# Where tiles start in SBUF: matmul operands at one place modulo 256 bytes, the gated halves staggered by 64

## The chip, the cores and the metric

The kernel runs on one core of a Trainium2 chip. The metric is device time in microseconds for one execution of the whole program. Each kernel's time is the median of several executions; the profile is of one further execution, taken by the hardware profiler. Its span runs from the first to the last instruction of the program, and the execution's own time is a little longer than its span.

## What is computed

A small two-way attention between tokens and state slots, followed by a gated feed-forward block with a three-tap convolution along the sequence. B, H, S, Ns, D are 8, 8, 512, 32, 64; the feed-forward block takes 512 features to 1024 and back.

```
scores = x @ state^T / 8;   a  = softmax(scores);   xread = a  @ state
scores2 = state @ x^T / 8;  a2 = softmax(scores2);  sread = a2 @ x
y = concat([xread, sread], axis=sequence)           # (B, 544, 512)
h = relu(y @ w_in)
conv = conv_w[0]*h[t-1] + conv_w[1]*h[t] + conv_w[2]*h[t+1]
out = (h * sigmoid(conv)) @ w_out
```

## The kernel before

All work is recorded as operations of one engine each (a matmul group, an activation, a vector operation, a load), and a table of numbers, `ORDER`, sets the order in which they are issued. No scheduler decides anything at build time, and each engine runs its list in that order, waiting on semaphores where an operand isn't ready.

The feed-forward block takes nearly all the time. It runs in 64 steps, i = 8b + f, for batch b and slice f of 128 of the 1024 hidden features. In a step:

- `hidden` (L579) multiplies: the stationary operand is a 128x128 piece of `u` (state times `w_in`), the moving operand 128x512 of `a` (the softmax). Both are kept as a high and a low half in float32r, `u0`/`u1` and `a0`/`a1`, and `PASSES` runs three products: u1 by a0, u0 by a1, u0 by a0, each over two groups, so six matmuls a step. In batch 0 plain float32 is used instead (L574, operands `u` and `p`).
- ScalarE applies relu into a tile `h` (L584), multiplies by the middle tap into a tile `t` (L601); VectorE adds the two other taps (L605, L610); ScalarE takes a tanh (L614); VectorE forms the gated value (L619).
- the gated value is split into halves `g0` (ScalarE, L178 through `gate_high`) and `g1` (VectorE, L181 through `gate_low`).
- `project` (L637 in `product`) multiplies: the stationary operand is a 128x128 piece of `g0` or `g1`, the moving one 128x512 of `wo` (the high or the low half of `w_out`), three passes for each of four chunks of the sequence, so twelve matmuls a step. The first four steps use plain float32 (L645, moving operand `whole`, stationary `t`). The same `product` serves the state rows (`gts` for `acc_t`) and the last chunk of batch 0 (`last` for `acc_c`).

In every matmul call the second argument is the stationary operand, which a LDWEIGHTS record (engine PEld in the profile) loads, and the third is the moving one, which the MATMUL record (engine PE) streams:

```
PE.matmul(acc, g[j][:, cs], wo[:, k, f, :], ...)          # L637
PE.matmul(ps_h[i], u[j][:, g, fs], a[k][:, g, :], ...)    # L579
```

There are 708 MATMULs of `g` with `wo`, 48 of `gts`, 24 of `last`, and 336 of `u` with `a`: 1116 in float32r, all with a stationary operand of 128 columns and a moving one of 512.

SBUF tiles come out of two pools, `keep` (one buffer for good) and `work` (a tag's buffers used in turn; `SBUF` gives their number: four `g0`, four `g1`, four `h`). A pool lays its tiles one after another in the order in which their tags first appear, so a tile's address follows from the sizes of those ahead of it. Two small sizes matter for what follows: `cw` is 96 bytes in a partition, and a tile `h` is 513 floats, 2052 bytes, and takes 2080.

Of the kernel before, what the change touches and what calls it, by code (L numbers as in the profile page):

```python
# [9 lines left out]
F32 = mybir.dt.float32  # L10
F32R = mybir.dt.float32r
# [4 lines left out]
P = 128  # L16
B, H, S, NS, D = 8, 8, 512, 32, 64
NP = H // 2
NG = H // 4
NCH = S // P  # L20
DM, DFF = 512, 1024
NK = DM // P
NF = DFF // P
T = S + NS

LOTS = ((0, 1, 2, 3), (4, 5, 6, 7))
# [16 lines left out]

SBUF = dict(hc=3, xt=4, xx=2, at=5, e2=2, e2t=2, af=1, a=2, u=2, h=4, t=5, g=4, ss=1,
            rr=2, nm2=4, s2=4, s1=4, o=2, gts=2)

RAW = ("a0", "a1", "u1")
PSUM = dict(acc=4, ph=2, ps=2)
# [103 lines left out]
def fused_kernel(ctx: ExitStack, tc: tile.TileContext, xT, xn, stT, w_in, conv_w, w_out, out):  # L152
    nc = tc.nc
    V, A, G, PE = nc.vector, nc.scalar, nc.gpsimd, nc.tensor

    psum = ctx.enter_context(tc.tile_pool(name="psum", bufs=4, space=bass.MemoryType.PSUM))
    keep = ctx.enter_context(tc.tile_pool(name="keep", bufs=1))
    work = ctx.enter_context(tc.tile_pool(name="work", bufs=2))

    def bank(name, tag="ps"):  # L160
        return psum.tile([P, 512], F32, tag=tag, name=name, bufs=PSUM[tag])

    def buf(shape, dtype, tag, name, pool=work, **kw):
        return pool.tile(shape, dtype, tag=tag, name=name, bufs=SBUF.get(tag) or SBUF[tag[:-1]], **kw)

    ident = keep.tile([P, P], F32, name="ident")
    make_identity(nc, ident)
    cw = keep.tile([P, NF, 3], F32, name="cw")
    wi = keep.tile([P, NK, DFF], F32, name="wi")
    wo = keep.tile([P, 2, NF, DM], F32R, name="wo")  # L170

    st = keep.tile([P, B * NP, NS], F32, name="st")

    sr = [keep.tile([P, NP, len(lot) * NS], F32, name=f"sr_{m}") for m, lot in enumerate(LOTS)]


    def high(hi, src):
# [24 lines left out]
    def w_tile(j, tag, *more):  # L202
        shape = [P, *pieces[j][0].shape[1:], *more]
        return buf(shape, U32, tag, f"{'raw' if more else tag}_{j}",
                   padded_shape=[P, *([1, 512] if j == W_CONV else shape[1:3]), *more])
# [18 lines left out]
    def w_sign(j):  # L224
        dst = pieces[j][1]
        if dst is None:
            f = j - W_OUT
            whole[f] = buf([P, DM], F32, f"g{f % 2}", f"whole_{f}")
            dst = whole[f].unsqueeze(1)
        V.scalar_tensor_tensor(dst.bitcast(U32), raws.pop(j)[:, :, :, 1], 0x80000000, hcs.pop(j),  # L230
                               op0=ALU.bitwise_and, op1=ALU.bitwise_or)
# [27 lines left out]
    at, ps_s, nm2, e2, ps_t, e2t, s2, ps_r, rr, ps_f, xts, xxs = ({} for _ in range(12))  # L259

    def xt_load(i):
        b, g = divmod(i, NG)
        xts[i] = buf([P, 2, S], F32, "xt", f"xt_{i}")
        nc.sync.dma_start(xts[i], xT[b, :, 2 * g:2 * g + 2, :])  # L264
# [99 lines left out]
    af, s1, av = {}, {}, {}  # L364
# [182 lines left out]
    corner = keep.tile([P, NF, 3], F32, name="corner")  # L547
    corner2 = keep.tile([P, NF, 3], F32, name="corner2")
    corners = keep.tile([P, 1, NF], F32, name="corners")
    last = keep.tile([P, NF, P], F32, name="last")  # L550

    def at_step(i):
        b, f = divmod(i, NF)
# [326 lines left out]
```

## Time and profile before

| | |
|---|---|
| median of three runs | 376.81 us |
| the three runs | 375.97, 378.32, 376.81 us |
| the profiled execution | 376.16 us |
| its span | 374.4 us |
| matmul records | 2418, as many weight loads |

How to read the profile's rows: in a row of a group stand the line, the engine, the operation, the tile written and the tiles read, the shape and the number of instructions. Matmul records overlap: each lasts from its start to the modelled end of its pipeline, so the time that one matmul takes from the engine is the distance from its start to the next one's start. The chain of work that ended last cuts its pieces at these starts, so that a piece's length divided by its count gives this distance.

### The profile page before, as it was taken

How to read it: one execution, taken by the hardware profiler on the slowest of the kernel's cores; microseconds unless marked ns; L12 is line 12 of the kernel's file. 1: busy time of each engine (PE TensorE's matmuls, PEld its weight loads, DVE VectorE, ACT ScalarE, POOL GpSimd, SP SyncE). 2: the span in 40 equal slices, each digit the busy share in tenths (PEclk: the TensorE clock that was granted, in tenths of full speed). 3: DMA queues.
4: the chain of work that ended last, by engine and by line, in shares of the span. 5: the costliest groups of instructions: out<-in, count | busy, mean ns of one | idle time of the engine just before them, and what ended most of it. 6: DMA issues, size and time to landing. Idle time of an engine off the chain costs nothing.

```text
span 374.4 us, 6509 instructions
## 1 busy us (share of the span) xinstructions
PE 362.8 (97%) x2418; PEld 267.4 (71%) x2418; DVE 309.2 (83%) x540; ACT 265.7 (71%) x536; POOL 44.2 (12%) x158
## 2 busy tenths in 40 slices
PE   7988989999999999999999999999999999999994
PEld 6852446677668776877888877877778778888883
DVE  1988999999999989989989898786787578666951
ACT  3898998866789689766765658666766477558632
POOL 1002102310121120102010011011311121011000
PEclk9999999999999999999999999999999999999998
DMA  7999984033310445000010011100020001002004
GB/s 257 326 355 312 379 290 166 0 114 100 141 43 2 144 141 190 34 2 4 28 56 2 0 56 58 56 4 15 13 86 0 28 30 56 2 0 86 3 0 168
DMA packets 21728, 35.05 MB, mean 94 GB/s; under 512 B 1600, under 2 KB 14272, under 8 KB 21696
## 3 DMA queue, kind: packets, MB, share of 16 engines
q1 hardware_dynamic: 21696, 34.63, 27.0%
q8 instruction: 19, 0.31, 0.4%
q14 instruction: 13, 0.11, 0.1%
HBM read 25.71 MB, written 8.91 MB: 92 GB/s over the span
## 4 chain that ended last, share of the span: by engine, by line
PE 89%; DMA 7%; SPq 2%; ACT 0%; issue 0%; ACTq 0%
PE acc L637 45%; PE ps_h L579 21%; PE ps_hs L560 4%; PE ps_u L494 4%; PE acc_t L637 3%; DMA raw<-w_in 3%; DMA st<-stT 3%; PE ps_h L574 2%; PE acc L645 2%; PE ps_r L318 2%; PE ps_s L277 2%; DMA xx<-xn 2%; PE acc_c L637 1%; PE ps_t L305 1%; SPq L209 1%; SPq L264 0%
## 5 line engine op out<-in xcount | busy, mean ns | idle before, releaser
L637 PE MATMUL acc<-wo,g 128*128 128x512 f32 x708 | 179.9, 400 | 0.0
L637 PEld LDWEIGHTS acc<-wo,g 128*128 128x128 f32 x708 | 131.0, 188 | 43.3 <-issue 8.4
L579 PE MATMUL ps_h<-a,u 128*128 128x512 f32 x336 | 85.7, 397 | 0.0
L579 PEld LDWEIGHTS ps_h<-a,u 128*128 128x128 f32 x336 | 62.4, 188 | 15.9 <-issue 1.7
L605 DVE SCALAR_TENSOR_TENSOR t<-h,cw,t 128x511 f32<-128x511 f32 x64 | 47.1, 744 | 11.0 <-ACT t L601 10.8
L584 ACT ACTIVATE h<-ps_h 128x512 f32<-128x512 f32 x64 | 37.8, 594 | 19.6 <-PE ps_h L579 12.9
L614 ACT ACTIVATE t<-t 128x512 f32<-128x512 f32 x64 | 39.6, 627 | 15.3 <-DVE t L610 15.2
L610 DVE SCALAR_TENSOR_TENSOR t<-h,cw,t 128x512 f32<-128x512 f32 (+1 forms) x64 | 47.3, 745 | 1.7 <-POOL h L589 0.5
L619 DVE SCALAR_TENSOR_TENSOR t<-t,h 128x512 f32<-128x512 f32 (+1 forms) x64 | 42.2, 666 | 5.8 <-ACT t L614 5.6
L181 DVE TENSOR_TENSOR g<-t,g 128x512 fp32r<-128x512 f32 (+1 forms) x60 | 40.2, 674 | 7.4 <-ACT g L178 7.1
L178 ACT ACTIVATE g<-t 128x512 fp32r<-128x512 f32 (+1 forms) x60 | 37.0, 621 | 11.9 <-DVE t L619 8.1
L601 ACT ACTIVATE t<-h,cw 128x512 f32<-128x512 f32 x64 | 44.7, 719 | 0.1
L589 POOL COPY h<-hs 128x1 f32<-128x1 f32 x56 | 20.3, 372 | 172.2 <-DVE t L619 141.9
L594 POOL COPY hs<-h 128x1 f32<-128x1 f32 x64 | 19.0, 315 | 120.3 <-ACT h L584 120.2
L651 ACT ACTIVATE o<-acc 128x512 f32<-128x512 f32 (+1 forms) x30 | 17.1, 584 | 11.6 <-PE acc L637 11.3
L181 DVE TENSOR_TENSOR u<-ps_u,u 128x512 fp32r<-128x512 f32 x28 | 18.6, 679 | 3.9 <-ACT u L178 3.9
L178 ACT ACTIVATE u<-ps_u 128x512 fp32r<-128x512 f32 x28 | 16.1, 594 | 4.2 <-PE ps_u L494 4.1
L188 PE MATMUL idle<-ident 128*128 128x128 f32 x102 | 14.8, 306 | 1.8 <-POOL ident masks.py:199 1.8
L560 PEld LDWEIGHTS ps_hs<-sr,wi 128*128 128x128 f32 x128 | 15.7, 191 | 1.2 <-ACT sr L333 0.4
L188 PEld LDWEIGHTS idle<-ident 128*128 128x128 f32 x102 | 13.7, 216 | 3.5 <-POOL ident masks.py:199 1.8
L213 ACT ACTIVATE hc<-raw 128x512 f32<-128x512 f32 (+1 forms) x17 | 11.1, 652 | 6.8 <-DMA raw<-conv_w 4.4
L560 PE MATMUL ps_hs<-sr,wi 128*128 128x128 f32 x128 | 15.7, 275 | 0.0
(88 smaller groups left out, 394.1 us busy)
## 6 DMA issues: line engine op xcount, KB each, us to landing
xt<-xT SPq DMA_DIRECT2D x16, 512.0 KB, 6.5
xx<-xn SPq DMA_DIRECT2D x16, 512.0 KB, 5.2
out<-o SPq DMA_DIRECT2D x30, 256.0 KB, 2.1
raw<-w_in SPq DMA_DIRECT2D x8, 512.0 KB, 7.1
raw<-w_out SPq DMA_DIRECT2D x8, 512.0 KB, 7.8
out<-o_t SPq DMA_DIRECT2D x8, 64.0 KB, 1.7
st<-stT SPq DMA_DIRECT2D x1, 448.0 KB, 10.4
out<-o_c SPq DMA_DIRECT2D x1, 256.0 KB, 6.7
```

The source lines that it names most:

```text
L178: A.activation(hi, src, AF.Copy)
L181: engine.tensor_tensor(lo, src, hi.bitcast(F32), op=ALU.subtract)
L188: PE.matmul(idle[0][:, :P], ident, ident, start=True, stop=True)
L560: PE.matmul(ps_hs[m, f][:, :NT], wi[:, k, f * P:(f + 1) * P], sr[m][:, k, :], start=(k == 0), stop=(k == NK - 1))
L579: PE.matmul(ps_h[i], u[j][:, g, fs], a[k][:, g, :], start=(n == 0), stop=(n == 3 * NG - 1))
L584: A.activation(hd[i][:, :S], ps_h.pop(i), AF.Relu, scale=0.5)
L601: A.activation(tt[i], hd[i][:, :S], AF.Copy, scale=cw[:, f, 1:2])
L605: V.scalar_tensor_tensor(t[:, 1:], h[:, :S - 1], cw[:, f, 0:1], t[:, 1:], op0=ALU.mult, op1=ALU.add)
L610: V.scalar_tensor_tensor(t[:, :n], h[:, 1:n + 1], cw[:, f, 2:3], t[:, :n], op0=ALU.mult, op1=ALU.add)
L614: A.activation(tt[i], tt[i], AF.Tanh, scale=0.25)
L619: V.scalar_tensor_tensor(tt[i][:, :n], tt[i][:, :n], 1.0, hd[i][:, :n], op0=ALU.add, op1=ALU.mult)
L637: PE.matmul(acc, g[j][:, cs], wo[:, k, f, :], start=(f == 0 and n == 0), stop=(f == NF - 1 and n == 2))
```

## The change

A third pool, `even`, is opened ahead of `keep` and `work`. Everything that a matmul reads, and nearly every other large tile, goes there; what stays in `keep` is `cw`, the tiles `hs` and three small ones, and in `work` the tags `h`, `nm2`, `s2` and `s1`, those whose sizes aren't whole multiples of 256 bytes or that no matmul reads. Tiles with the tags `g0` and `g1` (the gated halves, and `whole`, which borrows their buffers) are allocated with 16 floats more in a row, 2112 bytes in place of 2048; what is written and read in them is as before.

```diff
+STAGGERED = ("g0", "g1")
+UNEVEN = ("h", "nm2", "s2", "s1")
...
+    even = ctx.enter_context(tc.tile_pool(name="even", bufs=1))
     keep = ctx.enter_context(tc.tile_pool(name="keep", bufs=1))
     work = ctx.enter_context(tc.tile_pool(name="work", bufs=2))
...
-    def buf(shape, dtype, tag, name, pool=work, **kw):
-        return pool.tile(shape, dtype, tag=tag, name=name, bufs=SBUF.get(tag) or SBUF[tag[:-1]], **kw)
-
-    ident = keep.tile([P, P], F32, name="ident")
+    def buf(shape, dtype, tag, name, **kw):
+        if tag in STAGGERED:
+            kw["padded_shape"] = [P, S + 16]
+        return (work if tag in UNEVEN else even).tile(shape, dtype, tag=tag, name=name, bufs=SBUF.get(tag) or SBUF[tag[:-1]], **kw)
+
+    ident = even.tile([P, P], F32, name="ident")
...
-    wi = keep.tile([P, NK, DFF], F32, name="wi")
-    wo = keep.tile([P, 2, NF, DM], F32R, name="wo")
-
-    st = keep.tile([P, B * NP, NS], F32, name="st")
-
-    sr = [keep.tile([P, NP, len(lot) * NS], F32, name=f"sr_{m}") for m, lot in enumerate(LOTS)]
+    wi = even.tile([P, NK, DFF], F32, name="wi")
+    wo = even.tile([P, 2, NF, DM], F32R, name="wo")
+
+    st = even.tile([P, B * NP, NS], F32, name="st")
+
+    sr = [even.tile([P, NP, len(lot) * NS], F32, name=f"sr_{m}") for m, lot in enumerate(LOTS)]
...
-    last = keep.tile([P, NF, P], F32, name="last")
+    last = even.tile([P, NF, P], F32, name="last")
```

No operation is added, removed or moved: on every engine the instructions, their order, their shapes and the semaphores that they wait for are the same before and after. What differs is addresses, and the distance between rows of the gated halves. The tiles' start addresses modulo 256 bytes, as the two programs allocate them:

| tile | read by a matmul as | before | after |
|---|---|---|---|
| `wo` | moving, L637 | 224 | 128 |
| `g0`, `g1` | stationary, L637 | 64 | 128, 192, 0, 64 in turn |
| `gts` | stationary, L637 | 64 | 128 |
| `last` halves | stationary, L637 | 192 | 128 |
| `a0` | moving, L579 | 64 | 128 |
| `a1` | moving, L579 | 192 | 128 |
| `u0` | stationary, L579 | 192 | 128 |
| `u1` | stationary, L579 | 64 | 128 |
| `p`, `u` of batch 0 | moving, stationary, L574 | 192, 192 | 128, 128 |
| `whole`, `t` | moving, stationary, L645 | 64, 64 | 0, 64 or 128, and 128 |
| `wi`, `st`, `sr` | both, L494, L560, L277 | 224 | 128 |
| `xt`, `xx`, `e2t` | L277, L318 | 192 | 128 |
| `h` (no matmul) | | 192, 224, 0, 32 | 192, 224, 0, 32 |

The four buffers of `g0` and the four of `g1` run through the four places together, so both halves of one step lie at the same place. Counted from `wo`, a gated half lies 96 bytes past it before (modulo 256), and 0, 64, 128 or 192 after, a quarter of the steps each.

## The prediction

> **What bounds the kernel now.** I read the totals by engine first, then the chain of work that ended last, then its pieces in order of time, since a change of addresses can only show in how long an instruction takes.
>
> ```profile
> span 374.4 us, 6509 instructions
> PE 362.8 (97%) x2418; PEld 267.4 (71%) x2418; DVE 309.2 (83%) x540; ACT 265.7 (71%) x536; POOL 44.2 (12%) x158
> ...
> PE 89%; DMA 7%; SPq 2%; ACT 0%; issue 0%; ACTq 0%
> ```
>
> TensorE is 89% of the chain, DMA 7%, no other engine counts. Stretch by stretch (us, then busy time and count of PE, PEld, DVE, ACT, POOL, granted clock, DMA share, GB/s):
>
> ```profile
> 0.00:72.00 72.00, 65.16 (x674) 41.77 (x674) 60.27 (x124) 60.25 (x132) 7.75 (x39) 1.00 0.80 271
> 72.00:320.00 248.00, 248.00 (x1544) 186.09 (x1534) 214.97 (x347) 176.24 (x341) 32.96 (x106) 1.00 0.16 53
> 320.00:370.00 50.00, 49.60 (x212) 39.54 (x210) 33.92 (x70) 29.02 (x65) 3.47 (x14) 1.00 0.10 37
> ```
>
> From 72 to 370 us TensorE never waits for more than an instant, at full clock; only the first 72 us have a second limit, the loads (DMA share 0.80). So the end moves with the distance between matmuls, times their number. The chain's pieces give it (start, length, line, count):
>
> ```profile
> 58.60 1.72 PE ps_h L574 x4
> ...
> 62.56 0.86 PE acc L645 x2
> ...
> 83.45 5.59 PE acc_c L637 x24
> ...
> 262.30 2.78 PE ps_h L579 x12
> ...
> 301.09 2.78 PE ps_h L579 x12
> ...
> 324.62 9.85 PE acc L637 x42
> ...
> 353.44 4.21 PE acc L637 x18
> ...
> 368.20 1.42 PE acc_t L637 x6
> ```
>
> A matmul of L637 takes 9.85/42 = 234.5 or 4.21/18 = 233.9 ns, of `last` 5.59/24 = 232.9, of `gts` 1.42/6 = 237 (a piece that short is good to 2 ns), one of L579 2.78/12 = 231.7. A float32 record takes 1.72/4 = 430 ns, 0.86/2 = 430 for L645. Each float32 matmul of the code stands as two such records (16 calls at L574, 32 records); if each of those goes over the 512 columns twice, one way over them takes 215 ns. That is an estimate, and it leaves 17 to 19 ns in each float32r matmul unexplained. This is the only sum that a change of addresses could touch: 1116 matmuls, some 19 us.
>
> **The change, part by part.** Nothing is added, removed or moved on any engine or queue; the edits to the pools and the padding have one answer together, new addresses, and I go through who reads them.
>
> *L637, 780 matmuls.* While one matmul streams `wo`, the next one's weights are loaded:
>
> ```profile
> L637 PE MATMUL acc<-wo,g 128*128 128x512 f32 x708 | 179.9, 400 | 0.0
> L637 PEld LDWEIGHTS acc<-wo,g 128*128 128x128 f32 x708 | 131.0, 188 | 43.3 <-issue 8.4
> L579 PE MATMUL ps_h<-a,u 128*128 128x512 f32 x336 | 85.7, 397 | 0.0
> L579 PEld LDWEIGHTS ps_h<-a,u 128*128 128x128 f32 x336 | 62.4, 188 | 15.9 <-issue 1.7
> ...
> L318 PEld LDWEIGHTS ps_r<-xx,e2t 128*32 128x32 f32 x512 | 7.6, 110 | 5.1 <-ACT hc L213 1.9 <-ACT e2t L309 1.7 <-issue 0.4
> ```
>
> If the two reads get in each other's way, it should depend on how far apart they lie. The program of before holds several distances already. Stationary past moving, modulo 256: 96 for `g` and `gts`, 224 for `last`, and in L579, taking the weights loaded during each pass, 0 for two passes of three and 128 for the third. These give 234 to 237, 232.9 and 231.7 ns. So 0 and 128, half of the new places, are the cheapest pairs already seen, and 96 and 224 cost 1 to 3 ns more. The weight loads tell why so little shows: 32 columns take 110 ns and 128 take 188, so a column takes 78/96 = 0.81 ns (an estimate), while the moving operand passes a column in 234/512 = 0.46 ns. In the 104 ns of a load of 512 bytes the other read advances some 900: the distance slides by about 400 bytes, more than a full turn of 256, whatever it was at the start.
>
> For 64 and 192 (half of the steps, some 354 matmuls) no row exists. Bounds: nothing unexplained is left, 215 ns; or load and stream don't overlap at all, 234 + 188 = 422 ns. That is -6.7 to +66.6 us. I take the nearest rows, the four known distances, 232 to 235, since 64 and 192 lie between them.
>
> What may be left is `wo` itself, which moves from 224 to 128, from an odd multiple of 32 bytes to a multiple of 64, as `a0` and `a1` were. If that is why L579 is 2.3 ns faster than L637, 780 x 2.3 = 1.8 us go; if it is something else (L579 reloads the same weights in a third of its loads), none. I take half: -0.9 us.
>
> *L579, 336 matmuls.* All at distance 0 now, two thirds were. Bounds from rows: 230.8 (the shortest piece of twelve, 2.77 us, at 153.10) to 234.5: -0.3 to +0.9 us; I take 0.
>
> ```profile
> 153.10 2.77 PE ps_h L579 x12
> ```
>
> *Float32 matmuls.* L574 with both operands at 192 and L645 with both at 64 take the same 430 ns; 0 us, with 56 records and a resolution of 5 ns in a piece of two, +-0.3.
>
> *ScalarE and VectorE* read and write the moved tiles. Their operations on `h`, which lies at 192, 224, 0 and 32 in turn, tell what a place costs them (shortest, median, longest in ns):
>
> ```profile
> L605 DVE SCALAR_TENSOR_TENSOR t<-h,cw,t x64: 705/745/766, 31.1 to 351.2; 128x511 f32<-128x511 f32 x64
> ...
> L584 ACT ACTIVATE h<-ps_h x64: 572/598/626, 28.0 to 345.0; 128x512 f32<-128x512 f32 x64
> ```
>
> The four places fall within 4% of the median but for one or two ends; 0 us. Their cover is the 13% of VectorE's time left from 72 to 320 us (214.97 of 248); it is gone when each of the 347 operations there gets 95 ns longer.
>
> *Loads.* Targets were at 64, 192 and 224, now at 128. On the chain:
>
> ```profile
> 7.19 10.58 DMA raw<-w_in
> ...
> 20.23 10.37 DMA st<-stT
> ...
> 47.42 6.18 DMA xx<-xn
> ```
>
> 27.1 us in all. No row splits them by place. The nearest are two loads of 512 KB with their median us to landing, `xt` (at 192) and `w_in` (five buffers' turns of eight at 64, three at 192):
>
> ```profile
> xt<-xT SPq DMA_DIRECT2D x16, 512.0 KB, 6.5
> ...
> raw<-w_in SPq DMA_DIRECT2D x8, 512.0 KB, 7.1
> ```
>
> Were the whole difference due to place, 8% of 27.1 us would be 2.2 us either way. `w_in` also comes in pieces of 512 bytes and `xt` in longer ones, so I allow half for the range, +-1.1 us, and take 0.
>
> The sum: 376.16 - 0.9 = 375.3 us on the profiled execution. That execution lies 0.65 us under the median of 376.81, so on medians the same sum is 375.9. I forecast 375.6.
>
> [...]
>
> **The rivals.**
>
> *Faster: the unexplained 17 to 19 ns are a conflict between weight load and stream, and even places remove it.* For it speaks that the excess is in every float32r matmul and not in the float32 records, where stream and load are less pressed. Against it speaks that it is there at 0, 96, 128 and 224 alike, within 3 ns. All of it gone, 1116 x 18 = 20 us: 356. A half is likelier: 366. It counts as faster from 3.8/1116 = 3.4 ns a matmul.
>
> [...]
>
> *Slower: places that coincide collide.* A quarter of the `g` steps (177 matmuls), all of L579's remaining third (112), `gts` (48) and `last` (24) come to distance 0, 361 matmuls; with the stagger's 64 and 192, 354 more stand at distances never run here. For it speaks only that these are new. Against it: L579 has 224 of its 336 at 0 and is the fastest group. Priced at a second helping of 18 ns on 715 matmuls it is +12.9 us: 389. It decides from 3.8/715 = 5.3 ns each.
>
> *Slower on the vector side* would need the 95 ns above; I give it nothing of its own. That the addresses don't come out as meant is excluded by the allocation.
>
> **How the numbers follow.** About 1%, 3.8 us, is what a measurement of this kernel can tell from no change. No difference by place beyond a few ns: 0.80, with 375.6 us. Conflict removed, 366: 0.12. Collision, 389: 0.08. Within the likeliest case, the bounds from rows are -1.8 - 0.3 - 0.3 - 1.1 = -3.5 and +0.9 + 0.3 + 1.1 = +2.3 us, on 376.2 (the profiled execution) and on 376.8 (the median): 372.7 to 379.1. The three runs before spread by 2.4 us, so I open it a little, more on the side where a small part of the first rival would fall: 371.5 to 379.5. The two rivals beyond that, 0.2 at most, lie outside.
>
> **What would show it.** In the chain's pieces after: L637 per matmul within 231 to 236 ns and L579 within 230 to 235 says the main step is right; L637 at L579's value says the place of `wo` was the difference. L637 under 228 anywhere, or pieces of different steps that differ with i modulo 4 (the four staggered places), proves distance counts. Longer weight loads than 188 ns, or L584 and L605 off 598 and 745 ns, would prove it on the load side or on the other engines. A lower granted clock would make all this unreadable.

## The result, and the profile after

| | before | after |
|---|---|---|
| median of 17 runs | 377.46 us | 375.75 us |
| lowest and highest | 375.96, 381.54 | 373.73, 378.71 |
| span of the profiled execution | 374.4 us | 372.5 us |

The ratio of after to before is 0.9927, with a 95% interval of 0.9902 to 0.9951: by the paired ratio faster by about 2.8 us (1.7 us between the two medians). That is inside the 1% that was called no change, but the interval excludes 1: a small, real gain.

First the totals of the kernel after (by engine, then the chain), and two of its groups. The change moved the code by six lines: L643 is what was L637, L585 was L579.

```profile
span 372.5 us, 6509 instructions
...
PE 360.6 (97%) x2418; PEld 266.6 (72%) x2418; DVE 308.9 (83%) x540; ACT 265.6 (71%) x536; POOL 43.3 (12%) x158
...
PE 87%; DMA 9%; SPq 1%; ACT 1%; issue 0%; DVE 0%; ACTq 0%
...
L643 PE MATMUL acc<-wo,g 128*128 128x512 f32 x708 | 178.5, 398 | 0.0
L643 PEld LDWEIGHTS acc<-wo,g 128*128 128x128 f32 x708 | 130.7, 188 | 42.3 <-issue 9.2
L585 PE MATMUL ps_h<-a,u 128*128 128x512 f32 x336 | 84.8, 394 | 0.0
...
L590 ACT ACTIVATE h<-ps_h 128x512 f32<-128x512 f32 x64 | 37.9, 595 | 18.6 <-PE ps_h L585 11.6
```

TensorE's busy time fell from 362.8 to 360.6 us; on every other engine the change is under 1 us. The weight load still takes 188 ns. The chain's pieces after (start, length, what, count), those that answer to the pieces shown of before:

```profile
83.73 5.44 PE acc_c L643 x24
...
261.42 2.75 PE ps_h L585 x12
...
268.29 1.36 PE acc L643 x6
...
299.83 2.72 PE ps_h L585 x12
...
323.07 9.79 PE acc L643 x42
...
351.69 4.17 PE acc L643 x18
```

The 24 matmuls of the last chunk of batch 0, which are at distance 0 now, went from 232.9 to 226.7 ns each; hidden from 231.7 to between 226.7 and 229.2; the staggered projection in its long pieces only from 234 to 231.7 or 233. The short piece at 268.29, in which all weights stand at distance 0, took 1.36/6 = 226.7 ns a matmul. Start to start, and leaving out steps over 250 ns, at which another kind of matmul breaks in or TensorE waits, the trace's records give these means in ns:

| | before | after |
|---|---|---|
| projection (`g`) | 233.9 | 231.7 |
| hidden (`u`, `a`) | 231.8 | 228.9 |
| `gts` | 234.4 | 229.0 |
| `last` | 233.0 | 226.7 |

Summed over the 1075 places at which two float32r matmuls follow each other, 254.6 us became 252.0, 2.6 us less. From the start of the first float32r matmul to the start of the last, 296.83 us became 294.54, 2.29 us less. That is the measure used below, since it repeats to 0.02 us from execution to execution, while the 72 us ahead of it don't.

### The profile page after: what moved, and what is told of

It reads as the page before. It is cut to its first block, busy times and chain, and to the rows that moved or that the text cites. A ratio compares the mean times of both kernels' runs of the same rounds, so it can differ in the third digit from the quotient of the medians.

```text
span 372.5 us, 6509 instructions
## 1 busy us (share of the span) xinstructions
PE 360.6 (97%) x2418; PEld 266.6 (72%) x2418; DVE 308.9 (83%) x540; ACT 265.6 (71%) x536; POOL 43.3 (12%) x158
## 4 chain that ended last, share of the span: by engine, by line
PE 87%; DMA 9%; SPq 1%; ACT 1%; issue 0%; DVE 0%; ACTq 0%
PE acc L643 45%; PE ps_h L585 21%; PE ps_hs L566 4%; PE ps_u L500 4%; PE acc_t L643 3%; DMA st<-stT 3%; DMA raw<-w_in 3%; PE acc L651 2%; PE ps_r L324 2%; PE ps_s L283 2%; DMA raw<-w_out 2%; PE acc_c L643 1%; DMA xx<-xn 1%; PE ps_t L311 1%; PE ps_h L580 1%; SPq L215 1%
## 5 line engine op out<-in xcount | busy, mean ns | idle before, releaser
L643 PE MATMUL acc<-wo,g 128*128 128x512 f32 x708 | 178.5, 398 | 0.0
L643 PEld LDWEIGHTS acc<-wo,g 128*128 128x128 f32 x708 | 130.7, 188 | 42.3 <-issue 9.2
L585 PE MATMUL ps_h<-a,u 128*128 128x512 f32 x336 | 84.8, 394 | 0.0
L585 PEld LDWEIGHTS ps_h<-a,u 128*128 128x128 f32 x336 | 62.3, 188 | 15.3 <-issue 1.7
L600 POOL COPY hs<-h 128x1 f32<-128x1 f32 x64 | 17.9, 297 | 119.4 <-ACT h L590 119.3
```

The source lines that it names most:

```text
L585: PE.matmul(ps_h[i], u[j][:, g, fs], a[k][:, g, :], start=(n == 0), stop=(n == 3 * NG - 1))
L643: PE.matmul(acc, g[j][:, cs], wo[:, k, f, :], start=(f == 0 and n == 0), stop=(f == NF - 1 and n == 2))
```

## The experiments

Two theories stood after the result. Distance: what counts is how far the weights being loaded lie from the operand being streamed. Place: what counts is where the streamed operand starts by itself. In all kernels below the tiles are those of the changed kernel, so every matmul operand is at 128 modulo 256 but for what is said. The first four and the three repeats near the end ran several times, so that a ratio to the kernel before can be given; the other five ran once each, with a profile, and give spacings alone.

**Even, no staggering.**

```diff
-        if tag in STAGGERED:
-            kw["padded_shape"] = [P, S + 16]
```

> The staggering alone is taken back: the gated halves have 2048 bytes again and lie at 128 modulo 256, at distance 0 from their weights like every other matmul operand. Distance theory (a stream and a weight load that stand at the same place settle into a steady 226 to 227 ns, as the 24 matmuls of the last chunk of batch 0 do after the change; other distances keep them unsettled at 230 to 236): L637's matmuls fall from 231.4 to about 227 ns, those of hidden from 228.9 to about 227, some 4 us more than the change gave, a ratio to before of 0.980 to 0.985. Place theory (what helps is that the streamed operand starts at a multiple of 128 bytes): nothing changes against the changed kernel, 231 ns, ratio 0.993.

Measured: 374.05 us, ratio 0.9904 (0.9867 to 0.9941). The projection (L640 in this kernel) takes 228.0 ns, hidden 227.7. The pieces of the chain:

```profile
86.17 5.44 PE acc_c L640 x24
...
300.91 2.72 PE ps_h L582 x12
...
311.70 4.11 PE acc L640 x18
...
344.28 7.48 PE acc L640 x33
352.44 4.08 PE acc L640 x18
```

4.08/18, 7.48/33, 2.72/12 and 5.44/24 are all 226.7 ns. The distance theory's matmul times came true within 1 ns; the ratio stayed short of its range. Some 4 us more than the change were expected, and the stretch from first to last gained 1.9 us more, from 294.54 to 292.66; I come back to the reasons.

**Even, 64 bytes further, all operands at 192.**

```diff
+    front = ctx.enter_context(tc.tile_pool(name="front", bufs=1))
+    front.tile([P, 16], F32, name="gap0")
     even = ctx.enter_context(tc.tile_pool(name="even", bufs=1))
```

> Everything as in the kernel without staggering, but 64 bytes further: all operands at 192 modulo 256, distance 0. Distance theory: about 227 ns in both groups again, ratio 0.980 to 0.985. Place theory: a stream at an odd multiple of 64 costs what the second half of a at 192 cost before, 233 to 234 ns, ratio 0.998 to 1.002.

Measured: 374.71 us, ratio 0.9910 (0.9877 to 0.9944), projection 228.0 ns, hidden 227.8.

```profile
350.41 4.08 PE acc L642 x18
```

The same 4.08 us with the stream at an odd multiple of 64: the place theory falls.

**The gated halves at a fixed distance.** They get a pool of their own with a gap in front, of 32 floats for 128 bytes, and 24, 16, 48, 8 and 64 floats for the others. The gap also shifts the small tiles and `h` behind it, which no matmul reads.

```diff
+    gated = ctx.enter_context(tc.tile_pool(name="gated", bufs=1))
+    gated.tile([P, 32], F32, name="gap_gated")
...
+        return (gated if tag in ('g0', 'g1') else work if tag in UNEVEN else even).tile(...)
```

128 bytes:

> All even, but all the gated halves 128 bytes past the weights. Distance theory: L637 stays unsettled at 230 to 234 ns, hidden at 227 to 229, ratio about 0.993. Place theory (the streamed operand alone counts, and it is at 128): as without staggering. A theory in which the distance counts modulo 128 gives 227 ns here too, ratio 0.980 to 0.985.

96 bytes, as before the change:

> All even, but the gated halves 96 bytes past the weights, the distance that they had in the kernel before. Distance theory: L637 is back at 233 to 235 ns, hidden at 227 to 229, ratio 0.995 to 0.998. Place theory: 227 to 231 ns in L637, ratio 0.980 to 0.993.

64 bytes:

> All even, the gated halves 64 bytes past the weights in every step. If only distance 0 settles: L637 at 230 to 234 ns with hardly any matmul at 226 or 227, hidden at 228 to 230. If every multiple of 64 settles once it is kept for long enough: L637 at about 228, as without staggering.

192 bytes:

> All even, the gated halves 192 bytes past (64 short of) the weights in every step. If only distance 0 settles: L637 at 230 to 234 ns. In the changed kernel loads at this place stood at 230.5 ns on the mean with 18% at 226 or 227, more than the other staggered places, so that a second settling distance, at about 226 to 228, is possible here.

32 bytes:

> All even, the gated halves 32 bytes past the weights. If the distance counts by whether both lie in the same 64 bytes: about 228 ns as at 0. If only distance 0 settles: 230 to 235 ns in L637.

256 bytes, run last, since all the settled kernels were at 0 modulo 512 too:

> All even, the gated halves 256 bytes past the weights: distance 0 modulo 256, 256 modulo 512. In all the settled kernels so far the distance was 0 modulo 512 too. If the period is 256 (as the change has it): as without staggering, 228 ns in L637 and 4.08 us for the piece of 18 matmuls near 353 us. If it is 512: L637 unsettled at 229 to 234 ns, 4.12 to 4.21 us.

Measured, with the same piece of 18 projection matmuls near 353 us in each. First 128 bytes, then 96, 64, 192, 32 and 256:

```profile
355.06 4.20 PE acc L642 x18
```

```profile
354.41 4.21 PE acc L642 x18
```

```profile
354.97 4.20 PE acc L642 x18
```

```profile
351.43 4.12 PE acc L642 x18
```

```profile
355.93 4.20 PE acc L642 x18
```

```profile
352.10 4.08 PE acc L642 x18
```

| `g` past `wo`, bytes | projection, ns | hidden, ns | first to last, us | ratio to before |
|---|---|---|---|---|
| 0 (even) | 228.0 | 227.7 | 292.66 | 0.9904 (0.9867 to 0.9941) |
| 32 | 232.8 | 229.7 | 295.42 | |
| 64 | 233.3 | 229.5 | 295.54 | |
| 96 | 233.8 | 229.6 | 295.77 | 0.9972 (0.9942 to 1.0002) |
| 128 | 232.7 | 229.8 | 295.27 | 0.9961 (0.9932 to 0.9989) |
| 192 | 229.7 | 228.1 | 293.46 | |
| 256 | 228.0 | 227.8 | 292.69 | |
| 0 to 192 in turn (the change) | 231.7 | 228.9 | 294.54 | 0.9927 (0.9902 to 0.9951) |
| before | 233.9 | 231.8 | 296.83 | 1 |

`wo` stays in its place here, and the projection's time goes with where the gated halves lie: back to 234 at 96 as before the change, least at 0 and at 256. The place of the weights by itself is not what counts either: at 192 modulo 256 they gave 228.0 ns with `wo` at 192 too, and 233.3 with `wo` at 128 (the row for 64 bytes). 256 repeats 0 within 0.03 us, as a period of 256 asks. Three expectations were missed: hidden came out above the 227 to 229 foreseen at 96 and 128, the ratio at 128 above the 0.993, and 192, at 229.7 ns, between its two answers.

The single spacings show what is different at 0. In a long stretch of projection matmuls near 330 us (near 345 in the even kernel), in ns from start to start:

```
0 bytes    227 227 226 227 227 226 227 227 226
192        229 232 226 229 232 226 229 231 226
64         236 231 236 231 235 231 236 231 236
32         235 232 235 231 235 232 235 232 235
128        241 232 231 232 228 230 233 241 232 231 232 228 230 232
96         231 234 235 233 232 237 238 231 234 235 233 232 237 238
before     231 235 235 233 232 237 238 230 235 235 233 232 237 238
```

Each distance settles into a cycle of its own: of one matmul at 0, three at 192, two at 64 and 32, seven at 128 and 96, with a mean of 226.7, 228.9, 233.3, 233.3, 232.3 and 234.3 ns. The kernel before, also at 96 but with `wo` at 224 in place of 128, has the same cycle within 1 ns. And settling takes time. After another kind of matmul has broken in, or a wait, the even kernel gives much the same sequence, entered early or late, so that three to eleven matmuls pass before it is settled. Entered early, it is:

```
335 229 233 236 224 231 236 228 233 231 226 227 227 226 227
```

So staggering costs twice. Three quarters of the steps run at a distance with a longer cycle. And each step of twelve changes the distance, so that nothing stays settled for long: sorted by the distance of the weights being loaded, the matmuls of the change take 230.9, 232.3, 232.7 and 230.3 ns at 0, 64, 128 and 192, where distance 0 kept throughout gives 228.0. The hidden matmuls, all at distance 0 in both kernels, take 228.9 against 227.7. The mean of the four fixed distances, (228.0 + 233.3 + 232.7 + 229.7)/4 = 230.9, lies 0.8 under the 231.7 of the change.

**Hidden's two operands moved together.** Distance 0 in each group, but another place: `a` and `u` at 192, the projection's at 128.

```diff
+    hiddens = ctx.enter_context(tc.tile_pool(name="hiddens", bufs=1))
+    hiddens.tile([P, 16], F32, name="gap_hiddens")
...
+        return (hiddens if tag in ('a0', 'a1', 'u0', 'u1') else work if tag in UNEVEN else even).tile(...)
```

> All even, but both operands of hidden (a and u) together 64 bytes further, at 192, the projection's at 128: the distance is 0 in each group, the place changes between groups. Distance theory: both groups settle, 227 to 229 ns each with most at 226 or 227. A theory in which all successive matmuls must read at the same place: both groups are unsettled again, 229 to 232 ns, since the groups alternate every 6 to 12 matmuls.

```profile
302.27 2.76 PE ps_h L584 x12
...
354.00 4.08 PE acc L642 x18
```

Measured: neither as expected. The long piece of the projection settles (226.7), hidden doesn't: 2.76/12 = 230 ns, mean 230.0; projection 228.7. First to last is 293.59 us, 0.9 more than with one place. Going over from one group to the other unsettles the matmuls behind it although the distance within each group is 0, and hidden's runs of 6 to 12 seldom settle again: 21% of its spacings are 226 or 227 ns, against 78% in the even kernel. Whether the new place does this or the one load in between isn't told apart: the first weights of a group are loaded while the last matmul of the other group streams, at a distance of 64 or 192.

**Three kernels once more, on one chip:** before, even, and the change, with no edit.

> The kernel before once more, for its first 72 us beside those of the next two on one chip. In the earlier looks the first float32r matmul started at 72.4 us before, 72.7 after the change, and 73.1 to 76.2 in the eight kernels with even tiles. If even tiles slow the loads, this one starts near 72.4 and the two others 1 to 3 us later; if the loads differ from execution to execution and from chip to chip, this one lies among them. Its float32r matmuls repeat the sum of 254.6 us to 0.3 in either case. Ratio 1.000.

> Even without staggering once more: sum of the float32r matmuls' distances 249.6 us, 5.0 less than before; ratio 0.987 to 0.991, and below that of the change by 0.002 to 0.007 if what TensorE wins reaches the end.

> The change once more, beside the one without staggering: sum 252.0 us, ratio 0.991 to 0.995.

| | first float32r matmul starts, us | first to last, us | ratio to before |
|---|---|---|---|
| before | 74.97 | 296.85 | 0.9980 (0.9956 to 1.0004) |
| even | 74.76 | 292.68 | 0.9859 (0.9822 to 0.9897) |
| the change | 73.58 | 294.56 | 0.9909 (0.9875 to 0.9943) |

The kernel before started its first float32r matmul at 72.37 us in its first profile and at 74.97 in this one: the loads ahead differ that much by themselves, and no effect of the tiles on them can be told. The stretch behind repeats to 0.02 us for each kernel. Even without staggering beats both in first to last; its ratio lies under the change's both times (0.9904 and 0.9927, 0.9859 and 0.9909), but the intervals overlap, so in whole times the difference isn't shown for certain. Both repeated ratios lie just below what was expected of them.

**Why even wins 4.2 us where its matmuls win 5.0.** Their spacings sum to 249.6 us against 254.6, but the stretch from first to last shrinks by 4.2 us only. The other 0.8 us lies outside these 1075 spacings, nearly all of it at L563 (L560 before), the matmuls for the state rows, in two places near 194 and 217 us. The six steps from a projection matmul to one of L563 take 2.06 us together in place of 1.39, and those within its groups 6.43 in place of 6.22. What TensorE waits for there is ScalarE's copy out of an earlier result of L563, a wait that the kernel before doesn't have (us in total, times, longest):

```profile
PEld ps_hs L563 <- ACT hs L567: 1.2, 2, 0.7
```

A second new wait stands inside the 249.6 us. The shares of the chain show it first, since TensorE had 89% before:

```profile
PE 66%; DVE 16%; DMA 8%; ACT 6%; issue 3%; SPq 1%; DVEq 0%; ACTq 0%
```

Between 319 and 341 us, where TensorE stood in the chain of the kernel before, the chain of the even kernel runs over the engines that make the gated halves (pieces of it in that window):

```profile
317.85 1.37 PE ps_h L582 x6
...
321.62 1.29 DVE g L184 x2
322.91 0.66 DVE t L608
323.57 1.99 DVE t L613 x3
...
340.52 0.70 DVE g L184
341.22 0.04 issue
341.26 0.96 PE acc L640 x3
```

TensorE has caught up with them. Among the waits, before and then even:

```profile
PEld acc L637 <- DVE g L181: 0.8, 1, 0.8
```

```profile
PEld acc L640 <- DVE g L184: 3.6, 6, 0.8
```

Of these 2.8 us more the matmuls show 0.5 in four spacings near 331 and 341 us: 300, 335, 481 and 338 ns, 1.45 us together in place of 0.93.

## Why the prediction was right, and where its reasons weren't

The time, 375.6 forecast and 375.75 measured, and the class, no change beyond 1%, came out. That the two times agree within 0.2 us is luck: the gain was 2.3 us in the stretch of float32r matmuls, against the 0.9 forecast, and the kernel before had a median of 377.46 us over 17 runs, against the 376.81 over three from which the forecast started. The signs that the prediction set decide against its mechanism: hidden at 226.7 to 229.2 ns lies below its 230 to 235, and the piece of the projection at 268.29 us, at 226.7, lies under the 228 that was to prove that distance counts. By its steps:

- *What bounds it.* Right: the whole gain of the change is in the spacing of the float32r matmuls.
- *L637, -0.9 us.* Right in sign, with a wrong reason and too small: of the 2.6 us that the spacings won, about 1.7 are this line's. The step that failed is "the distance slides by about 400 bytes, more than a full turn of 256, whatever it was at the start", an estimate from the lengths of two weight loads (110 and 188 ns) and the spacing of 234 ns, from which 0, 64, 128 and 192 were to be alike. The runs gave 228.0, 233.3, 232.7 and 229.7 ns. The rows quoted for distance 0, hidden's before, were no fair sample: its streams changed place between 64 and 192 from pass to pass, and a third of its loads stood at 128, so that it hardly ever settled (3% of its spacings are 226 or 227 ns). The -0.9 itself was given to the start of `wo` moving to a multiple of 64; with `wo` there and `g` at 96 the projection takes 233.8 ns, as before, so that is worth nothing.
- *L579, 0 us, bounds -0.3 to +0.9.* Missed below: 231.8 to 228.9 ns, some 0.9 us over the 318 spacings. The bounds came from rows of the kernel before, in which no group with all its operands at one place existed to be seen.
- *Float32, ScalarE and VectorE at 0.* No difference seen: a float32 record stands 429 ns from the next at L574 in both kernels (the median), a relu took 595 ns against 594, and VectorE was busy for 308.9 us against 309.2.
- *Loads at 0, within 1.1 us.* The start of the first float32r matmul varies by 2.6 us between two executions of the kernel before, so the term can't be checked; the bound of 1.1 us was too narrow for one execution.
- *Rival "conflict removed".* Its mechanism is nearer to what was found than the forecast's: the distance between load and stream does set the spacing. But of the 19 ns over the estimate of 215 only 7.6 go, even at distance 0 in a settled stretch (234.3 to 226.7), and nothing here shows what the other 12 are. The 215 itself is half of the 430 ns between float32 records, on the supposition that each record goes over the columns twice; no run shows that, and the spacing never came under 226.7 ns in a settled stretch.
- *Rival "coinciding places collide".* The reverse: distance 0 is the best of the distances tried, with 228.0 ns in the projection (256 repeats it) against 229.7 to 233.8 at the others.
- *The four distances before, alike within 3 ns.* In the prediction this spoke against a conflict. Measured in settled stretches the distances differ by 7.6 ns, from 226.7 at 0 to 234.3 at 96, so that where the weights lie against the stream does count.

The class was right since the true effect, 2.3 us in the stretch, is small against 376, and since the change contains a gain and nearly half its undoing: even tiles are worth 296.83 - 292.66 = 4.2 us, and the staggering gives 1.9 of them back.

What stays open is the cause: the runs show that the spacing goes with the distance between weights and stream, and not why. Distances that aren't multiples of 32 bytes weren't tried, nor were 160 and 224 in the projection, nor operands of another type or size.

## What to carry to other kernels

Where TensorE runs without gaps and loads weights for each matmul, as it did here from 72 to 370 us, try all tiles that its matmuls read at one place modulo 256 bytes (here all at 128 or all at 192, each with 228.0 ns in the projection): keep tiles of other sizes (here one of 96 bytes and one of 2052) in a pool behind them, and don't pad. It took each matmul of a settled stretch from 234.3 to 226.7 ns here (3.2%; float32r, weights of 128 columns, 512 streamed), shortened the whole kernel by about 1%, and costs no instruction (6509 before, after and in the even kernel). In the profile, look at spacings in long runs of one kind, not at means over a mixed trace: before the change hidden took 231.8 ns on the mean although two thirds of its loads stood at distance 0, while its streams changed place from pass to pass, and 227.7 with all tiles at one place.

## What the hardware showed that was not expected

The spacing of this kernel's projection matmuls is in long stretches a cycle that repeats within 1 ns and goes with the distance between weights and stream: 226.7 ns at 0 and 256 bytes, 228.9 at 192, 232.3 at 128, 233.3 at 32 and at 64, 234.3 at 96. After an interruption three to eleven matmuls pass, at 224 to 240 ns each behind the break itself, before the even kernel falls into it.
